# One GpSimd weight split a tile in the first mixture, and a shorter, padded balancing loop in the second routing

## The chip, the core and the metric

The kernel runs on one core of a Trainium2 chip. A core has five engines with queues of their own: TensorE (PE in the rows; its weight loads are PEld), VectorE (DVE), ScalarE (ACT), GpSimd (POOL) and SyncE (SP, which only issues transfers here). The metric is device time in microseconds (us).

## The reference, cut to what matters

Three layers follow each other: attention whose scores under a row's threshold are dropped, a mixture of eight experts in which every token goes to the expert of its largest logit, and a second mixture in which (token, expert) pairs are taken in falling order of their logits and each expert takes at most 288 tokens.

```python
e_idx = np.argmax(logits, axis=1)                  # first mixture
h = np.maximum(x[mask] @ w1[e], 0.0)
out[mask] = gate_w[mask, None] * eom[mask, e, None] * (h @ w2[e])
...
cap = N // E                                       # second mixture: 2304 // 8
order = np.argsort(-logits.flatten())
for idx in order:
    tok, e = idx // E, idx % E
    if assigned[tok] >= 0 or counts[e] >= cap: continue
    assigned[tok] = e; counts[e] += 1
out[mask] = np.maximum(x[mask] @ w1[e], 0.0) @ w2[e]
```

## The kernel before

All work is in program order on each engine; the order is written out by hand in Python, and engines wait for each other by semaphores that the framework places.

**First mixture (`moe1`).** The tokens are sorted by expert into tiles of 128; with these inputs tiles 0 to 22 run (tiles 23 and 24 stand in a branch that is not taken). A tile needs eight weight chunks of 128 x 1024: c = 0 to 3 for the first product (`mm1`), c = 4 to 7 for the second (`mm2`). Products are made in split precision: `split(t,c)` makes `wh`, a rounded copy of the raw chunk (ScalarE, L609), and `wl`, the rest raw - wh (a subtraction, L610 on GpSimd or L611 on VectorE). Which engine subtracts is the condition in L610: before, GpSimd does c = 2 from tile 3 on, c = 5 from tile 1 on and c = 7 from tile 2 on; VectorE does the others. Once `wl` is there, SyncE's `prefetch` may load the next expert's chunk into the same buffer.

`splits(n)` lets the splits run up to n chunks ahead of those TensorE has used, and seven buffers hold split chunks. Worked out from `order` and from the calls of `splits`, an iteration t of the steady loop puts this into VectorE's queue: the splits (t,4), (t,5), (t,6); then `ey(t-1)`, which scales the second product of the tile before out of PSUM into `y` (L667); then two `hl` (L650, low parts of the turned activations, out of PSUM); then the splits (t,7), (t+2,0); then `xl` (L621, out of PSUM); then the splits (t+2,1), (t+2,2), (t+2,3). Of these, the ones that GpSimd makes go into its queue instead, between its `gather` calls (L615, indirect loads of tokens). TensorE's queue in the same iteration: the first half of `mm1(t+1)`, the transposes `Th` of `hT(t)` (L647), the second half of `mm1(t+1)`, the transposes `Ty` of `y` (L673), the transposes `Tx` of the next tokens (L619), `mm2(t)` (L660 to L662), and in every second iteration the next router's logits. In tile t = 20 to 22 `reach` adds a maximum over all logits, with a small copy `fmb` (L696) on VectorE.

**Second routing (`route2`).** Six iterations look for each expert's threshold at once. In each, VectorE compares the current scores with 33 levels (`G`, L832), TensorE counts (`cn`, 25 small products, L836), VectorE marks the levels whose count is at least 288 (`gp`), TensorE sums the marks of each expert onto all partitions (`sp`, L858), and VectorE derives a step `s` and a factor `f` from `sp` (L861, L862, L864, L866; 8 columns each), shifts and scales the scores (`D`, `Qe`, `U`) and takes the new choice `O`. Beside it, in iterations 1 to 4 (counted from 0), TensorE and ScalarE split weight chunks of the second mixture (`split_pe`, two half chunks an iteration, written to `Tw`), and `busy(n)` issues n products of 512 columns whose result nobody reads. After the loop `rows` ranks the chosen tokens (26 products, L876 and L877), builds one-hot rows (`OT`, `OR`) and multiplies them into token indices (L900), with which GpSimd gathers the tokens of the first expert (L995).

**Second mixture (`moe2`).** It begins with `busy(10)` (L1043), then transposes the gathered tokens (L1001) and multiplies, eight experts with three tiles of 96 tokens each.

Of the kernel before, what the change touches and what calls it, by code (L numbers as in the profile page):

```python
# [9 lines left out]
F32 = mybir.dt.float32  # L10
F32R = mybir.dt.float32r
BF16 = mybir.dt.bfloat16
I32 = mybir.dt.int32
AF = mybir.ActivationFunctionType
ALU = mybir.AluOpType
AX = mybir.AxisListType
ET = mybir.EngineType
P = 128
# [24 lines left out]
class Route:  # L43
# [8 lines left out]
    def T(self, nm, sh, dt=F32):  # L52
        return self.p.tile([P]+sh,dt,name=nm)
# [506 lines left out]
def moe1(tc, K, r, rts, xd, w1, w2, wg2, ys, LG2, reach_, ahead):  # L560
# [3 lines left out]
    nc=tc.nc; ident=K['ident']; N=NT1  # L564
    with ExitStack() as ctx:
# [7 lines left out]
        def rv(c,par): return raw[c][:,ds(par,1),:].rearrange("p a f -> p (a f)")  # L573
# [25 lines left out]
        def prefetch(t,c):  # L599
            q=regs[t]; nc.sync.dma_start(rvd(c,q['o']),src(q['n'],c),cond=q['c'],cond_hint=(t%3==0))  # L600
# [6 lines left out]
        def split(t,c):  # L607
            q=regs[t]; h,l=wtile()
            nc.scalar.copy(h,rv(c,q['a']))  # L609
            if t>(2 if c==2 else 0 if c==5 else 1 if c==7 else N): nc.gpsimd.tensor_sub(l,rv(c,q['p']),h.bitcast(F32))  # L610
            else: nc.vector.tensor_sub(l,rv(c,q['v']),h.bitcast(F32))  # L611
            prefetch(t,c); W[t,c]=(h,l)
        def gather(t):
# [97 lines left out]
        def splits(ahead):  # L711

            nonlocal pos
            while pos<min(used+ahead,ends[cur[0]]):
                t,c=order[pos]; pos+=1
                if c==0: regload(t)
                if t==0 and c<6: prefetch(t,c)
                else: split(t,c)
# [58 lines left out]
def route2_ahead(tc, K, A, ix, vs):  # L777

    V=tc.nc.vector; T=lambda nm,sh,dt=F32: K['cst'].tile([P]+sh,dt,name=nm)
    inv=T("inv",[1]); V.tensor_scalar_max(inv,A,1.0e-30); V.reciprocal(inv,inv); V.tensor_scalar_mul(inv,inv,KC/1.5)  # L780
    vb=T("vb",[NT1]); V.tensor_scalar(vb,vs,1.0,-1.0,op0=ALU.subtract,op1=ALU.mult)
    i2=T("i2",[2,NT1],I32); V.tensor_scalar(i2[:,0],ix,4,None,op0=ALU.arith_shift_right); V.tensor_scalar(i2[:,1],ix,15,None,op0=ALU.bitwise_and)
    f3=T("f3",[2,NT1]); V.tensor_copy(f3,i2)
    return vb,f3,inv


def route2(tc, K, LG2, A, ix, vs):
# [9 lines left out]
    nc=tc.nc; cst=K['cst']; V=nc.vector; g=nc.gpsimd; ident=K['ident']; K1=KC+1  # L797
    it2=K['it2']
    with ExitStack() as ctx:
        def pool(name,bufs,space=None):  # L800
            return ctx.enter_context(tc.tile_pool(name=name,bufs=bufs,side='right',reuse_waits="tile",**({'space':bass.MemoryType.PSUM} if space else {})))
        p=pool("r2",1)
        T=lambda nm,sh,dt=F32: p.tile([P]+sh,dt,name=nm)
        M8=lambda a: a.unsqueeze(2).to_broadcast([P,NT1,8])
        E8=lambda a: a.unsqueeze(1).to_broadcast([P,NT1,8])
        OH=T("OH",[26,8],BF16); g.memset(OH[:,25],0.0); O=OH[:,:NT1]
        Q=T("Q",[NT1,9]); g.memset(Q[:,:,8:9],0.5); Qe=Q[:,:,:8]

        rtile=yield
        vb,f3,inv=route2_ahead(tc,K,A,ix,vs)  # L810
        mn=T("mn",[NT1]); U=T("U",[NT1,8]); D=T("D",[NT1,8]); u=T("u",[NT1]); G=T("G2",[NT1,K1],BF16)
# [9 lines left out]
        def want0(w=ALL): s_=slice(*w); V.tensor_reduce(mn[:,s_],Q[:,s_],axis=AX.X,op=ALU.min)  # L821
        def want1(w=ALL): s_=slice(*w); V.tensor_tensor(O[:,s_],Qe[:,s_],W(mn,w,8),op=ALU.is_equal)
        def begin(w):
            s_=slice(*w)
            V.scalar_tensor_tensor(Qe[:,s_],LG2[:,s_],-TINY,W(vb,w,8),op0=ALU.mult,op1=ALU.add)
            V.tensor_scalar(U[:,s_],LG2[:,s_],A,inv,op0=ALU.add,op1=ALU.mult)
            want0(w); want1(w)
# [9 lines left out]
        def counts(cn,w):  # L837
            for z in looks(w): count((cn,*w),z)
# [5 lines left out]
        split,fetch=yield  # L844
        ps=pool("r2p",2,1)
        begin((EARLY,NT1))
        gp=p.tile([K1,8],BF16,name="gp"); s=T("s",[8]); f=T("f",[8]); f1=T("f1",[8]); f2=T("f2",[8])
        def busy(n):

            w=ps.tile([P,512],F32,tag="s",name="w")  # L850
            for _ in range(n): nc.tensor.matmul(w,K['onesb'],K['onesb'].unsqueeze(1).to_broadcast([P,4,P]),start=True,stop=True)
        def iteration(extra=0,warm=0,first=False):

            cn=ps.tile([K1,8],F32,tag="s",name="cn")
            counts(cn,(EARLY,NT1) if first else ALL)
            if first: V.scalar_tensor_tensor(gp,cn,287.5,nA,op0=ALU.subtract,op1=ALU.is_ge)
            else: V.tensor_scalar(gp,cn,287.5,None,op0=ALU.is_ge)
            sp=ps.tile([P,8],F32,tag="s",name="sp"); nc.tensor.matmul(sp,K['onesb'][:K1],gp,start=True,stop=True)  # L858
            for _ in range(extra): next(split)
            if warm: busy(warm)  # L860
            V.tensor_scalar(s,sp,1.0,0.0,op0=ALU.subtract,op1=ALU.max)  # L861
            V.tensor_scalar(f1,sp,KC+0.5,0.5-ZOOM,op0=ALU.is_ge,op1=ALU.mult)  # L862
            V.tensor_sub(D,U,E8(s))
            V.tensor_scalar(f2,sp,0.5,1.0-ZOOM,op0=ALU.is_lt,op1=ALU.mult)  # L864
            V.scalar_tensor_tensor(Qe,D,0.0,Qe,op0=ALU.is_lt,op1=ALU.add)
            V.scalar_tensor_tensor(f,f1,ZOOM,f2,op0=ALU.add,op1=ALU.add)  # L866
            want0()
            V.tensor_mul(U,D,E8(f))
            want1()
        ee=T("ee",[NT1]); sa=T("sa",[NT1,8]); rk=T("rk2",[NT1]); rw=T("rw",[NT1]); q1=T("q1",[NT1]); q2=T("q2",[NT1]); tt=T("tt",[NT1])  # L870
        OT=T("OT",[NT1,4,24],BF16); OR=T("OR",[NT1,96],BF16); sc=T("sc",[2,24]); Rr=[None]; n8=T("n8",[8]); dn=T("dn",[8]); fl=T("fl",[1]); fi2=T("fi2",[1],I32)
# [2 lines left out]
        def ranks():  # L874
            r=Rr[0]=ps.tile([P,26,8],F32,tag="R",bufs=1,name="R")
            nc.tensor.matmul(r,K['tri'],OH,start=True,stop=False,skip_group_check=True)  # L876
            for c in range(NT1): nc.tensor.matmul(r[:,c+1:],K['onesb'],OH[:,c:c+1].to_broadcast([P,NT1-c,8]),start=False,stop=c==NT1-1,skip_group_check=True)  # L877
        def rows(flag):

            ranks()  # L880
            V.tensor_mul(D,O,io8); V.tensor_reduce(ee,D,axis=AX.X,op=ALU.add)
            V.tensor_scalar_mul(e3,vb,-99.0); V.scalar_tensor_tensor(e3,ee,3.0,e3,op0=ALU.mult,op1=ALU.add)
            r=Rr[0]
            V.tensor_mul(sa,r[:,:25],O)
            if flag: V.tensor_scalar(dn,r[:,25],288.0,None,op0=ALU.not_equal)
            V.tensor_reduce(rk,sa,axis=AX.X,op=ALU.add)
            if flag: V.tensor_reduce(fl,dn,axis=AX.X,op=ALU.max)
            V.tensor_scalar(q1,rk,95.5,None,op0=ALU.is_ge)
            if flag: V.tensor_copy(fi2,fl)
            V.scalar_tensor_tensor(q2,rk,191.5,q1,op0=ALU.is_ge,op1=ALU.add)  # L890
            V.tensor_add(tt,e3,q2)
            V.scalar_tensor_tensor(rw,q2,-96.0,rk,op0=ALU.mult,op1=ALU.add)
            def hot(eng,t0,t1): eng.tensor_tensor(OR[:,t0:t1],io96[:,:96].unsqueeze(1).to_broadcast([P,t1-t0,96]),rw[:,t0:t1].unsqueeze(2).to_broadcast([P,t1-t0,96]),op=ALU.is_equal)
            V.tensor_tensor(OT[:,:,2],K['iota'][:,:24].unsqueeze(1).to_broadcast([P,NT1,24]),b24(tt),op=ALU.is_equal)
            io96=ps.tile([P,96],F32,tag="s",name="io96"); V.tensor_copy(io96,K['iota'][:,:96])
            g.tensor_mul(OT[:,:,0],OT[:,:,2],b24(K['iota'][:,:NT1]))
            nc.scalar.activation(OT[:,:,1],OT[:,:,2],AF.Copy,scale=K['pf'])
            for t in (0,5,10,15,20): hot(V,t,t+5)
            IX=ps.tile([96,2,24],F32,tag="s",name="IX2")
            for c in range(NT1): nc.tensor.matmul(IX,OR[:,c],OT[:,c,0:2],start=c==0,stop=c==NT1-1)  # L900
            V.tensor_copy(sc[:96],IX)
            V.scalar_tensor_tensor(it2[:96,0],sc[:96,0],128.0,sc[:96,1],op0=ALU.mult,op1=ALU.add)
# [8 lines left out]
        def greedy(c8):  # L911
# [18 lines left out]
                V.tensor_scalar(pen,pen,NBIG,None,op0=ALU.mult)  # L930
                V.tensor_add(L,L,M8(pen)); V.tensor_add(L,L,E8(cl))
            V.tensor_copy(O,oh)
        for j in range(6): iteration(2 if 1<=j<5 else 0,0 if j<5 else 5,j==0)
        rows(True); fetch(False)
        flag=lambda: nc.values_load(fi2[0:1,0:1],min_val=0,max_val=1)>0

# [13 lines left out]
def moe2(tc, K, ys, w1, w2, out):  # L950
# [3 lines left out]
    nc=tc.nc; ident=K['ident']  # L954
    with ExitStack() as ctx:
# [41 lines left out]
        def xT(e,i):  # L997
            if i==0: XT[e]=(xp.tile([P,4,288],F32R,tag="xh",name="xh"),xp.tile([P,4,288],F32R,tag="xl",name="xl"))
            h,l=XT[e]; x=X.pop((e,i)); s=slice(i*96,i*96+96)
            p=psT.tile([P,4,96],F32,tag="T",name="Tx")  # L1000
            for c in range(4): nc.tensor.transpose(p[:,c].bitcast(F32R),x[:,c*P:(c+1)*P],K['identr'][:96,:96])  # L1001
            nc.scalar.copy(h[:,:,s],p); nc.vector.tensor_sub(l[:,:,s],p,h[:,:,s].bitcast(F32))  # L1002
# [37 lines left out]
        def busy(n):  # L1040

            w=psT.tile([P,512],F32,tag="T",name="w")
            for _ in range(n): nc.tensor.matmul(w,K['onesb'],K['onesb'].unsqueeze(1).to_broadcast([P,4,P]),start=True,stop=True)  # L1043
        busy(10)
        for i in range(3): xT(0,i); busy(3 if i<2 else 2)
        splits(6); loads(14)
        for e in range(8):
# [83 lines left out]
```

## Time and profile before

| | |
|---|---|
| median of 3 runs | 946.09 us (945.7 to 946.3) |
| the profiled execution's own time | 945.42 us |
| its span, first to last instruction | 943.6 us |
| mean granted TensorE clock | 0.981 of full speed |
| busy: PE, DVE, ACT, POOL | 886.3, 725.2, 635.6, 384.7 us |

The span is what the rows are placed in: times in them are us from its start. Attention fills it to about 321 us, the first mixture to 657, the second routing to 704, the second mixture the rest. An engine's busy time is an average over stages with different limits, so it is read by stage.

### The profile page before, as it was taken

The numbers are of one execution on the slowest core, as the hardware profiler recorded it, in microseconds if no ns is written. First come the engines' busy times: TensorE is split into PE (matmuls) and PEld (weight loads), VectorE is DVE, ScalarE is ACT, GpSimd is POOL, SyncE is SP. The second block draws the span as 40 slices with busy tenths as digits, with TensorE's granted clock in tenths as the row PEclk, the third lists the DMA queues.
The fourth block names the chain that finished last, engine by engine and source line by source line (L and its number), as shares of the span: only waits on it lengthen the run. The fifth ranks groups of instructions, "written<-read, shape, count | busy, mean of one in ns | idle before, by whom it ended". The sixth has DMA issues, their size and how long they took to land. (4 is left out here: it accounts for less than half of the span.)

```text
span 943.6 us, 18044 instructions
## 1 busy us (share of the span) xinstructions
PE 886.3 (94%) x5939; PEld 733.2 (78%) x5939; DVE 725.2 (77%) x1191; ACT 635.6 (67%) x1070; POOL 384.7 (41%) x391
## 2 busy tenths in 40 slices
PE   7899999999999999899999999998779999999995
PEld 6677777777777667678787777786449999999994
DVE  5898988888888789798999998987755555555540
ACT  5787878878977677677787788774315555555541
POOL 4234323433431324577777776774030221122211
PEclk9999999999999999999999999999779999999998
DMA  7534444544331670155544655111535666666500
GB/s 190 149 88 124 122 118 115 130 128 115 104 83 53 221 259 25 44 163 185 170 154 148 211 168 182 43 36 46 180 117 180 194 192 186 179 193 203 162 26 25
DMA packets 69346, 127.64 MB, mean 135 GB/s; under 512 B 14912, under 2 KB 27200, under 8 KB 69248
## 3 DMA queue, kind: packets, MB, share of 16 engines
q1 hardware_dynamic: 64016, 109.91, 38.4%
q0 software_dynamic: 5232, 16.52, 5.6%
q8 instruction: 49, 0.80, 0.4%
q14 instruction: 49, 0.40, 0.1%
HBM read 159.70 MB, written 15.99 MB: 186 GB/s over the span
## 5 line engine op out<-in xcount | busy, mean ns | idle before, releaser
L611 DVE TENSOR_TENSOR wl<-raw,wh 128x1024 fp32r<-128x1024 f32 x115 | 218.1, 1916 | 28.4 <-ACT wh L609 28.1
L610 POOL TENSOR_TENSOR wl<-raw,wh 128x1024 fp32r<-128x1024 f32 x63 | 167.6, 2662 | 102.2 <-ACT wh L609 101.4
L609 ACT CAST wh<-raw 128x1024 fp32r x178 | 177.7, 1064 | 4.0 <-PE Y L662 3.3
L469 ACT ACTIVATE e<-S,nm 128x576 f32<-128x576 f32 x144 | 107.8, 749 | 55.0 <-DVE nm L464 54.6
L464 DVE TENSOR_REDUCE nm<-S 128x1 f32<-128x576 f32 x144 | 108.4, 757 | 21.8 <-PE S L388 10.6
L499 DVE SCALAR_TENSOR_TENSOR a<-S,th,e 128x576 f32<-128x576 f32 x144 | 114.4, 814 | 11.1 <-ACT e L469 4.8
L966 DVE TENSOR_TENSOR wl<-raw,wh 128x1024 fp32r<-128x1024 f32 x60 | 73.4, 1225 | 36.9 <-ACT wh L966 36.9
L1037 POOL DMA_INDIRECT out_dram<-o,it x24 | 22.4, 934 | 173.0 <-ACT o L1031 154.1
L397 PE MATMUL T<-ident,a 128*128 128x128 f32 x576 | 86.6, 273 | 0.0
L1008 PE MATMUL H<-xh,wh 128*128 128x288 f32 x256 | 77.8, 304 | 0.1
L1020 PE MATMUL Y<-hh,wh 128*128 128x288 f32 x256 | 77.5, 303 | 0.0
L318 POOL TENSOR_TENSOR ql<-f,QH 64x512 fp32r<-64x512 f32 x30 | 38.2, 1274 | 94.5 <-ACT f L317 76.4
L419 PE MATMUL O<-aT,v 128*64 128x288 f32 x512 | 75.8, 418 | 0.5 <-ACT xt L424 0.5
L1009 PE MATMUL H<-xl,wh 128*128 128x288 f32 x256 | 75.6, 295 | 0.2 <-DVE xl L1002 0.2
L633 PE MATMUL H<-wh,xh 128*128 128x512 f32 x184 | 75.1, 408 | 0.7 <-ACT xh L621 0.7
L1021 PE MATMUL Y<-hl,wh 128*128 128x288 f32 x256 | 75.5, 295 | 0.0
L1022 PE MATMUL Y<-hh,wl 128*128 128x288 f32 x256 | 75.5, 295 | 0.0
L402 ACT COPY aT<-T 128x512 f32<-128x512 f32 x128 | 75.2, 588 | 0.2 <-PE T L397 0.2
L660 PE MATMUL Y<-wh,hh 128*128 128x512 f32 x184 | 74.5, 405 | 0.9 <-ACT wh L609 0.9
L1010 PE MATMUL H<-xh,wl 128*128 128x288 f32 x256 | 75.3, 294 | 0.0
L662 PE MATMUL Y<-wh,hl 128*128 128x512 f32 x184 | 72.3, 393 | 0.0
L661 PE MATMUL Y<-wl,hh 128*128 128x512 f32 x184 | 72.3, 393 | 0.0
(344 smaller groups left out, 2130.4 us busy)
## 6 DMA issues: line engine op xcount, KB each, us to landing
raw<-in_moe_w_dram SPq DMA_DIRECT2D x256, 512.0 KB
ys<-y SPq DMA_DIRECT2D x23, 256.0 KB
q<-in_q_dram SPq DMA_DIRECT2D x16, 256.0 KB
k<-in_k_dram SPq DMA_DIRECT2D x16, 256.0 KB
v<-in_v_dram SPq DMA_DIRECT2D x16, 256.0 KB
QA<-QH SPq DMA_DIRECT2D x32, 128.0 KB
QB<-QH SPq DMA_DIRECT2D x32, 128.0 KB
xd<-xr SPq DMA_DIRECT2D x16, 256.0 KB
```

The costliest lines, as they stand in the source:

```text
L397: for kb in (2*part,2*part+1): nc.tensor.transpose(TT[n][:,kb,:],a[:,o+kb*P:o+(kb+1)*P],ident)
L419: nc.tensor.matmul(O[hd*64:hd*64+64,:288],L['v'][:,hd,kb,:],aT[hd][:,kb,cs],start=kb==0,stop=False,skip_group_check=True)
L464: nc.vector.tensor_reduce(nm[:,i:i+1],S[i][:,:,:288],axis=AX.XY,op=ALU.max,negate=True)
L469: nc.scalar.activation(e[i],S[i][:,:,:288],AF.Exp,bias=nm[:,i:i+1])
L499: nc.vector.scalar_tensor_tensor(a[:,hd*576:hd*576+576].rearrange("p (a b) -> p a b",a=2),S[i][:,:,:288],th[:,i:i+1],e[i],op0=ALU.is_ge,op ...
L609: nc.scalar.copy(h,rv(c,q['a']))
L610: if t>(2 if c==2 else 0 if c==5 else 1 if c==7 else N): nc.gpsimd.tensor_sub(l,rv(c,q['p']),h.bitcast(F32))
L611: else: nc.vector.tensor_sub(l,rv(c,q['v']),h.bitcast(F32))
L1008: nc.tensor.matmul(H[:,:288],wh[:,fs],xh[:,kc],start=kc==0,stop=False)
L1009: nc.tensor.matmul(H[:,:288],wh[:,fs],xl[:,kc],start=False,stop=False)
L1020: nc.tensor.matmul(Y[:,:288],wh[:,ds_],h,start=f==0,stop=False)
L1021: nc.tensor.matmul(Y[:,:288],wh[:,ds_],l,start=False,stop=False)
```

## The change

In the first mixture GpSimd makes one subtraction a tile: c = 5 in tile 1, c = 6 in later tiles. All others go to VectorE.

In the second routing a constant matrix `SF` is written once by GpSimd. Two products of its columns with `gp`, into two halves of `sp`, now give the step and the factor less one; the four small VectorE instructions that derived `s` and `f` go, and `D` and `U` read `sp` in PSUM. Three `busy` counts change: 3 more in iteration 4, 8 new after the ranks, and 16 for 10 ahead of the second mixture.

```diff
-            if t>(2 if c==2 else 0 if c==5 else 1 if c==7 else N): nc.gpsimd.tensor_sub(l,rv(c,q['p']),h.bitcast(F32))
+            if t>0 and c==(5 if t==1 else 6): nc.gpsimd.tensor_sub(l,rv(c,q['p']),h.bitcast(F32))
             else: nc.vector.tensor_sub(l,rv(c,q['v']),h.bitcast(F32))
...
+        SF=p.tile([K1,2,P],BF16,name="SF"); g.memset(SF[:,0],1.0); g.memset(SF[:1,0],0.0)
+        g.memset(SF[:,1],0.0); g.memset(SF[:1,1],ZOOM-1.0); g.memset(SF[KC:K1,1],0.5-ZOOM)
...
-            sp=ps.tile([P,8],F32,tag="s",name="sp"); nc.tensor.matmul(sp,K['onesb'][:K1],gp,start=True,stop=True)
+            sp=ps.tile([P,2,8],F32,tag="s",name="sp")
+            for x in range(2): nc.tensor.matmul(sp[:,x],SF[:,x],gp,start=True,stop=True)
             for _ in range(extra): next(split)
             if warm: busy(warm)
-            V.tensor_scalar(s,sp,1.0,0.0,op0=ALU.subtract,op1=ALU.max)
-            V.tensor_scalar(f1,sp,KC+0.5,0.5-ZOOM,op0=ALU.is_ge,op1=ALU.mult)
-            V.tensor_sub(D,U,E8(s))
-            V.tensor_scalar(f2,sp,0.5,1.0-ZOOM,op0=ALU.is_lt,op1=ALU.mult)
+            V.tensor_sub(D,U,E8(sp[:,0]))
             V.scalar_tensor_tensor(Qe,D,0.0,Qe,op0=ALU.is_lt,op1=ALU.add)
-            V.scalar_tensor_tensor(f,f1,ZOOM,f2,op0=ALU.add,op1=ALU.add)
             want0()
-            V.tensor_mul(U,D,E8(f))
+            V.scalar_tensor_tensor(U,E8(sp[:,1]),1.0,D,op0=ALU.add,op1=ALU.mult)
             want1()
...
             ranks()
+            if flag: busy(8)
...
-        for j in range(6): iteration(2 if 1<=j<5 else 0,0 if j<5 else 5,j==0)
+        for j in range(6): iteration(2 if 1<=j<5 else 0,(0,0,0,0,3,5)[j],j==0)
...
-        busy(10)
+        busy(16)
```

## Rows read from the trace of the kernel before

**Rows 1.** Busy us by stretch: PE, PEld, DVE, ACT, POOL (instructions), PEclk, DMA share, GB/s

```profile
382.00:383.00 1.00, 1.00 (x4) 0.81 (x3) 1.00 (x2) 1.00 (x2) 0.00 (x0) 0.50 0.78 293
...
510.00:540.00 30.00, 29.71 (x153) 23.95 (x152) 27.65 (x21) 23.84 (x31) 22.46 (x10) 1.00 0.61 208
...
720.00:740.00 20.00, 20.00 (x162) 19.99 (x161) 9.63 (x14) 9.26 (x17) 0.94 (x1) 1.00 0.45 134
```

**Rows 2.** TensorE's waits, 390 to 650 us: total, times, longest

```profile
PE Ty L673 <- DVE y L667: 2.0, 9, 0.2
PE Tx L619 <- DVE hl L650: 1.9, 2, 1.4
```

**Rows 3.** Groups by line, 380 to 665 us: busy, mean ns, idle before

```profile
L611 DVE TENSOR_TENSOR wl<-raw,wh 128x1024 fp32r<-128x1024 f32 x97 | 190.6, 1979 | 26.6 <-ACT wh L609 26.3
```

**Rows 4.** VectorE's timeline around tiles 1 and 2: start, length, operation

```profile
355.18 4.62 DVE L611 TENSOR_TENSOR wl<-raw,wh 128x1024 fp32r<-128x1024 f32 x4
...
367.40 12.32 DVE L611 TENSOR_TENSOR wl<-raw,wh 128x1024 fp32r<-128x1024 f32 x5
379.65 0.74 DVE L667 TENSOR_SCALAR y<-Y,gs 128x512 f32<-128x512 f32 x1
```

**Rows 5.** GpSimd's timeline, the same stretch

```profile
368.44 2.43 POOL L610 TENSOR_TENSOR wl<-raw,wh 128x1024 fp32r<-128x1024 f32 x1 [3.85 <-ACT wh L609]
...
376.01 2.63 POOL L610 TENSOR_TENSOR wl<-raw,wh 128x1024 fp32r<-128x1024 f32 x1 [0.67 <-ACT wh L609]
```

**Rows 6.** ScalarE's timeline, the same stretch

```profile
370.82 2.94 ACT L609 CAST wh<-raw 128x1024 fp32r x3
```

**Rows 7.** TensorE's timeline, the same stretch; idle before in brackets

```profile
380.53 0.63 PE L673 MATMUL Ty<-ident,y 128*128 128x128 f32 x4 [3.46 <-DVE y L667]
...
381.44 0.76 PE L660 MATMUL Y<-wh,hh 128*128 128x512 f32 x1
...
384.89 0.39 PE L662 MATMUL Y<-wh,hl 128*128 128x512 f32 x1
```

**Rows 8.** VectorE's timeline in later tiles

```profile
422.12 0.74 DVE L667 TENSOR_SCALAR y<-Y,gs 128x512 f32<-128x512 f32 x1
422.78 1.27 DVE L650 TENSOR_TENSOR hl<-Th,hh 128x512 fp32r<-128x512 f32 x2
...
425.46 0.68 DVE L621 TENSOR_TENSOR xl<-Tx,xh 128x512 fp32r<-128x512 f32 x1
...
639.13 1.42 DVE L696 COPY fmb<-fm 1x128 f32<-1x128 f32 x1
```

**Rows 9.** GpSimd's timeline beside the first of them

```profile
421.75 2.70 POOL L610 TENSOR_TENSOR wl<-raw,wh 128x1024 fp32r<-128x1024 f32 x1 [0.63 <-ACT wh L609]
```

**Rows 10.** TensorE's timeline in later tiles, two iterations apart

```profile
423.01 0.63 PE L673 MATMUL Ty<-ident,y 128*128 128x128 f32 x4 [0.22 <-DVE y L667]
...
449.99 0.63 PE L673 MATMUL Ty<-ident,y 128*128 128x128 f32 x4 [0.21 <-DVE y L667]
```

**Rows 11.** VectorE in the second routing

```profile
673.53 0.17 DVE L861 TENSOR_SCALAR s<-sp 128x8 f32<-128x8 f32 x1 [0.25 <-PE sp L858]
...
673.74 0.37 DVE L863 TENSOR_TENSOR D<-U,s 128x200 f32<-128x200 f32 x1
...
674.14 0.37 DVE L865 SCALAR_TENSOR_TENSOR Q<-D,Q 128x200 f32<-128x200 f32 x1
...
692.64 0.37 DVE L884 TENSOR_TENSOR sa<-R,OH 128x200 f32<-128x200 f32 x1 [1.17 <-PE R L877]
```

**Rows 12.** TensorE in the second routing and at the head of the second mixture

```profile
671.57 0.80 PE L974 MATMUL Tw<-wh,identm 128*128 128x512 f32 x1
672.30 0.79 PE L836 MATMUL cn<-OH,G 128*33 128x8 bf16 x25
...
699.33 3.73 PE L1043 MATMUL w<-onesb 128*128 128x512 bf16 x10 [0.69 <-PEq L937]
704.16 0.53 PE L1001 MATMUL Tx<-identr,x 96*128 96x96 f32 x4 [1.10 <-DMA x<-ys,it]
```

More of the change, by code (lines that the diff above doesn't have):

```diff
@@ L846, in route2 @@
         begin((EARLY,NT1))
-        gp=p.tile([K1,8],BF16,name="gp"); s=T("s",[8]); f=T("f",[8]); f1=T("f1",[8]); f2=T("f2",[8])
+        gp=p.tile([K1,8],BF16,name="gp")
         def busy(n):
```

## The prediction

> **What bounds the kernel now.** First read the busy times by stretch. In a steady stretch of the first mixture TensorE is busy 29.71 of 30 us, and in the second mixture 20.00 of 20 [rows 1]. VectorE has 27.65 of 30 us in the first and GpSimd 22.46 [rows 1]. So TensorE is the bound in both, and a change of the subtractions pays only where TensorE waits for VectorE. TensorE's list of waits says where that is: between 390 and 650 us nine short waits for `y`, 2.0 us in all, and two for `hl`, 1.9 us, of which one is 1.4 [rows 2]. Ahead of that stretch one wait is larger than all of these: in tile 2 `Ty` stands 3.46 us idle for `y` [rows 7]. After it the clock is at 0.50, the 1.2 GHz level [rows 1]. The gap before it is the only idle time in the stretch.
>
> VectorE's timeline tells why `y` is late. Four subtractions with GpSimd quiet take 4.62 us, 1.155 each; the five ahead of `y` take 12.32 us, 2.46 each [rows 4]. Beside those five GpSimd makes three of its own, the first from 368.44, the last from 376.01 to 378.64 [rows 5]. Five at 1.155 are 5.8 us, so 6.5 us were lost to three subtractions of about 2.5 us each: I read it as the two engines' subtractions taking turns, a whole instruction at a time. What reads PSUM is not held up: `y` ran 0.74 us inside a GpSimd subtraction of 2.70 (421.75 to 424.45) [rows 8, 9], as long as after the third one had ended [rows 4].
>
> **The change part by part: the first mixture.** GpSimd loses two of its three subtractions a tile, VectorE gets them. Hand walk of tile 2 with the queue order of the code, from the same start, 367.40 [rows 4]: VectorE makes (3,0) to (3,3), all four now, at 1.155, to 372.0. ScalarE's copies for (2,4), (2,5), (2,6) end at about 371.8, 372.8 and 373.8 [rows 6], so VectorE makes (2,4) to 373.2 and (2,5) to 374.35. Then comes `y`, because (2,6) is GpSimd's: it is done at about 375.1 instead of 380.4. TensorE was ready for it at 380.53 - 3.46 = 377.07 [rows 7], so the wait goes, 3.46 us. What is late next: `hl` needs 1.27 us behind `y` and is ready at 376.4; GpSimd's (2,6) runs from 374.35 to about 376.8 under `y` and `hl`, which read PSUM; (2,7) follows to about 378.0, and the second product, which uses it last, would start at 377.07 + (381.44 - 380.53) = 378.0 and needs (2,7) more than 3 us later. Nothing takes the wait's place. The slow clock behind it goes too: from 381.44 nine products, to the start of the one at 384.89, took 3.45 us [rows 7]. At twice the clock they would take at best half, 1.7; some part of a start-to-start time may not scale, so I take 2.1 (bounds 1.7 and 3.45), a gain of 1.35, and for the eight transposes ahead of them, between 380.53 and 381.44, another 0.2. Tile 2: 5.0 us. Bounds: 0, if the turns are no turns, to 5.4.
>
> Later tiles. In the order of the code two subtractions stand ahead of `y` in VectorE's queue before and after; after, none of them has to take turns with GpSimd's (t,5). The nine waits of 0.2 us should go: 1.8 us. In tile 21 the copy `fmb` took 1.42 us, one row of 128 numbers, beside a GpSimd subtraction, and `hl` behind it made TensorE wait 1.4 [rows 2, 8]. There GpSimd's (21,6) will still be running when `fmb` comes, but by my walk VectorE gets to `y` some 2 us sooner, and the wait goes: 1.4 us, bounds 0 to 1.6.
>
> What the added work costs VectorE: seven at 1.155 are 8.1 us a tile, `hl`, `y` and `xl` 2.7 [rows 8], together 10.8. A tile lasts (449.99 - 423.01)/2 = 13.5 us [rows 10]. One GpSimd subtraction can hold VectorE up by 2.5 us at most, which makes 13.3: still hidden under TensorE, though by a hair. I take 11 to 12, since the GpSimd one falls under `y` and `hl`. ScalarE's copies, the loads and the gathers keep their number and order. Sum for the first mixture: 5.0 + 1.8 + 1.4 = 8.2 us saved.
>
> **The second routing.** Between the end of `sp` and `D` stand `s` and the first part of `f`: `D` starts 673.74 - 673.53 = 0.21 us after `s` [rows 11]. The other two small ones are worth nothing: `Qe` starts at 674.14, just when `D`, which it needs, has ended (674.11) [rows 11], so the small one in between filled a wait. That bounds the gain to 0 to 6 x 0.21 = 1.26 us. It is not had where TensorE comes last: in iteration 2 the counts start at 672.30, behind a weight split from 671.57 of 0.80 us [rows 12], and iteration 4 has the same clock phase; so I count four of six, 0.84. Against it stands the second product. The 25 counts take 0.79 us with their weight loads, 0.03 each [rows 12]; if `D` waits for both products, six cost 0.2; as the upper bound one could take the delay of a whole small instruction, 0.16, six times 1.0. I take 0.25, nearest to the counts. The memsets of `SF` are GpSimd's and come when it has nothing else.
>
> `D` and `U` now read `sp` from PSUM. `sa` reads 200 columns of PSUM in 0.37 us, `D` on SBUF takes 0.37 [rows 11], so I cost that at nothing. The Trainium skill speaks against it: Perfetto Trace Analysis, section Optimizing Scalar/DVE Operations, gives VectorE about 60 ns of overhead an instruction on SBUF and about 125 on PSUM. By that rule the sum would be about 0.8 us worse (estimate from that page: twelve instructions at 65 ns). Here the rows decide, and they show no difference.
>
> The dummies. Ten of them ran 3.73 us from 699.33, to 703.06, and the gathered tokens let TensorE go on at 704.16, after 1.10 idle [rows 12]. 512 columns are 0.43 us at 1.2 GHz and 0.21 at 2.4, and the mean of the ten is 0.37, so some three of them ran at the upper level, which I place last. Six more end at 704.3 (all at the upper level) to 705.6 (all at the lower). I take 0.2 us of cost, bounds 0.1 to 1.5. The 8 after the ranks stand where TensorE has nothing to do until the one-hot rows are made, the 3 of iteration 4 between the splits and the counts. They may leave the ranks and L900 at the higher clock; I take 0.3 us for that, bounds -0.3 to 0.9.
>
> Sum for the routing: 0.84 - 0.25 - 0.2 + 0.3 = 0.7 us saved. Altogether 8.9 us off a span of 943.6: 934.7. The execution's own time was 945.42, 1.8 more than its span, and the median of the runs is 946.09, 0.7 above that: 934.7 + 1.8 + 0.3 (half the distance) = 936.8.
>
> **The rivals.** *Another wait takes the place of the tile-2 wait* (its products wait for tokens or for `hl`, or the clock falls all the same): the gain of tile 2 is 0 to 2, the time 940 to 942. For it: the stretch is crowded, with ScalarE copying in long rows [rows 6]. Against it: the walk leaves over 1 us for each.
>
> *The routing gives back*: the dummies hold TensorE past the tokens (1.5) and the second product costs its upper bound (1.0): 2.2 us worse than my sum, 939.
>
> *VectorE becomes the bound in the first mixture*: slower. A subtraction on VectorE takes 1.98 us on average now [rows 3]. If that is not turns but a general slowness beside GpSimd, loads and ScalarE, seven take more than a tile allows as soon as their mean is above (13.5 - 2.7)/7 = 1.54 us. At 1.7 a tile is 1.1 us longer, over 20 tiles 22 us: 959 with the rest. For it: 27.65 of 30 us busy before [rows 1]. Against it: 1.155 each wherever GpSimd is quiet [rows 4].
>
> *It does nothing*: the short waits stay and the clock costs what it cost, within 2 us of 946.1.
>
> **How the numbers follow.** Forecast 0.62, tile 2 filled otherwise 0.15, routing gives back 0.10, VectorE the bound 0.07, nothing 0.06. Faster by over 0.2%, which is about what a measurement of this kernel can tell from no change (1.9 us): 0.62 + 0.15 + 0.10 = 0.87; within it 0.06; slower 0.07. The range leaves out the slower cases and takes in the others: below the forecast 3 us (the upper bounds of the routing, 1.26 + 0.9 without the costs, and the waits' bounds), above it to 942.5.
>
> **What would show it.** VectorE's mean subtraction falls from 1.98 to 1.3 us or less with about 137 instead of 97 in that stretch; `Ty` in tile 2 has no idle time in front and the clock stays at full speed to 386; the nine waits are gone; the first mixture ends some 8 us sooner; `D` follows `sp` directly, and `Tx` of the second mixture still waits for its tokens, not for dummies. I am wrong if VectorE shows no idle time in the steady stretch, or if `Tx` starts right behind `busy(16)`.

## The result and the profile after

The changed kernel takes 932.76 us (median; 929.19 to 934.29) against 946.19 (945.7 to 947.32) for the kernel before on the same chip: ratio 0.9851, 95% interval 0.9831 to 0.9872, 13.4 us less. The forecast was 936.8 with a range from about 3 us below it to 942.5: the direction was right and the gain lies where it was looked for, in the first mixture, but it was larger than the range allowed. The profiled execution is the slowest of its four: 934.29 us, with a span of 932.3 against 943.6.

The views that answer to those of before follow in the same order. First the busy times by stretch (answering [rows 1]; columns as there):

```profile
382.00:383.00 1.00, 1.00 (x5) 0.56 (x3) 1.00 (x2) 0.00 (x0) 0.00 (x0) 1.00 0.00 0
510.00:540.00 30.00, 30.00 (x156) 24.59 (x155) 25.43 (x27) 24.64 (x33) 8.54 (x4) 1.00 0.51 176
```

VectorE makes far more subtractions and is busy for less time, 25.43 of 30 us instead of 27.65. The groups by line, 380 to 665 us, say why (answering [rows 3]): the mean falls from 1979 to 1258 ns, while GpSimd's own stays long.

```profile
L611 DVE TENSOR_TENSOR wl<-raw,wh 128x1024 fp32r<-128x1024 f32 x135 | 163.0, 1258 | 22.1 <-ACT wh L609 19.4 <-DMA raw<-in_moe_w_dram 0.3
L610 POOL TENSOR_TENSOR wl<-raw,wh 128x1024 fp32r<-128x1024 f32 x20 | 58.3, 2916 | 167.1 <-PE Th L647 86.7 <-ACT wh L609 60.8 <-issue 19.5
```

TensorE's waits, 390 to 650 us (answering [rows 2]): the nine short ones for `y` are gone, and there is a new one of 1.1 us in tile 22 (the list names `A`, a small copy that stands right behind `y` in VectorE's queue). The other two belong to the last tile, which lay behind 650 us before.

```profile
PE Ty L673 <- DVE A L698: 1.1, 1, 1.1
PE Ty L673 <- DVEq L765: 1.0, 1, 1.0
PE L L689 <- issue: 0.7, 1, 0.7
```

Tile 2 on VectorE's timeline (answering [rows 4]):

```profile
367.53 6.89 DVE L611 TENSOR_TENSOR wl<-raw,wh 128x1024 fp32r<-128x1024 f32 x6
374.34 0.74 DVE L667 TENSOR_SCALAR y<-Y,gs 128x512 f32<-128x512 f32 x1
375.00 1.28 DVE L650 TENSOR_TENSOR hl<-Th,hh 128x512 fp32r<-128x512 f32 x2
376.20 2.72 DVE L611 TENSOR_TENSOR wl<-raw,wh 128x1024 fp32r<-128x1024 f32 x2
```

GpSimd's timeline beside it (answering [rows 5]):

```profile
373.98 2.71 POOL L610 TENSOR_TENSOR wl<-raw,wh 128x1024 fp32r<-128x1024 f32 x1 [9.44 <-ACT wh L609]
```

and TensorE's (answering [rows 7]):

```profile
376.42 0.39 PE L635 MATMUL H<-wh,xl 128*128 128x512 f32 x1
376.65 0.60 PE L673 MATMUL Ty<-ident,y 128*128 128x128 f32 x4
...
377.38 0.46 PE L660 MATMUL Y<-wh,hh 128*128 128x512 f32 x1
```

Six subtractions take 6.89 us, 1.15 each, where five took 12.32. `y` starts at 374.34 instead of 379.65, under GpSimd's one subtraction, and `Ty` starts with no idle time in front.

**Where the time went.** The start of `Ty` marks each tile, so the distances between such rows show where the 11.3 us of span went. Worked out from the starts of `Ty` in both traces (tile by tile, us):

| stretch | before | after | gain | forecast |
|---|---|---|---|---|
| `Ty` of the first tile to the third (holds tile 2's wait) | 10.83 + 15.52 | 6.81 + 13.44 | 6.1 | 5.0 |
| third to twenty-first, 18 distances | 243.10 | 235.99 | 7.1 | 1.8 |
| twenty-first to last, 2 distances | 9.57 + 8.90 | 9.15 + 10.26 | -0.9 | 1.4 |
| last `Ty` to the first `Tx` of the second mixture (routing) | 46.54 | 47.35 | -0.8 | 0.7 |

They add up to 11.5; the first `Ty` itself comes 0.1 later. The 10.26 is of this execution: in the four other profiled kernels with the same first mixture it is 8.63 or 8.64, so this profile shows 1.6 us less gain than they do. The large surprise is the second line.

The steady loop is best read at the same tile in both. Before, `Ty` at 423.01 is the row of [rows 10], with 0.22 us idle listed in front. TensorE's timeline around it, before:

```profile
422.40 0.39 PE L635 MATMUL H<-wh,xl 128*128 128x512 f32 x1
...
423.51 0.54 PE L619 MATMUL Tx<-identr,x 128*128 128x128 f32 x4
424.11 0.44 PE L684 MATMUL Tl<-ident,ls 128*128 128x128 f32 x2
424.30 0.48 PE L660 MATMUL Y<-wh,hh 128*128 128x512 f32 x1
```

and after:

```profile
416.07 0.40 PE L635 MATMUL H<-wh,xl 128*128 128x512 f32 x1
416.31 0.60 PE L673 MATMUL Ty<-ident,y 128*128 128x128 f32 x4
416.67 0.54 PE L619 MATMUL Tx<-identr,x 128*128 128x128 f32 x4
417.04 0.40 PE L684 MATMUL Tl<-ident,ls 128*128 128x128 f32 x2
417.20 0.48 PE L660 MATMUL Y<-wh,hh 128*128 128x512 f32 x1
```

From the last `H` product to the first `Y` product it is 1.90 us before and 1.13 after: 0.77 lost, of which the list of waits showed 0.22. From `L635` to `Ty` 0.61 against 0.24: 0.37. `Ty` to `Tx` 0.50 against 0.36 and `Tx` to `Tl` 0.60 against 0.37: another 0.37, the rest at `Y`. The second part has its cause in [rows 8]: the two `hl` stand behind the late `y` in VectorE's queue, 422.78 to 424.05, and `Tx` and `Tl` start as the first and the second end. In the code `Th`, `Ty`, `Tx` and `Tl` take turns in the buffers of one PSUM tag, so a late `hl`, which reads `Th`, is a late buffer. And `y` is late for the same reason as in tile 2: the subtraction ahead of it takes its turn with GpSimd's. VectorE's timeline before shows it,

```profile
419.52 2.68 DVE L611 TENSOR_TENSOR wl<-raw,wh 128x1024 fp32r<-128x1024 f32 x1 [0.67 <-ACT wh L609]
```

with GpSimd's beside it:

```profile
418.63 2.49 POOL L610 TENSOR_TENSOR wl<-raw,wh 128x1024 fp32r<-128x1024 f32 x1 [2.68 <-ACT wh L609]
```

Nowhere else in the 106 rows of TensorE's timeline for these two tiles do before and after drift apart by more than 0.04 us. So each pair of tiles took 27.0 us (13.80 and 13.20) and takes 26.22 (13.43 and 12.79): nine pairs at 0.78 are the 7.1.

The list of what TensorE's weight loads wait for would have pointed there. Before, 390 to 650 us:

```profile
PEld Ty L673 <- ACT wh L609: 5.5, 9, 0.6
...
PEld Tl L684 <- DVE hl L650: 2.1, 10, 0.2
```

5.5 and 2.1 make 7.6, near the 7.1 gained; after, the first row is gone and the second is 0.2 us, once. The list is a pointer and no price: a single wait is 0.6 and 0.2 in it, where the two parts lost 0.37 and 0.40. (The first row names ScalarE's copies; in the tile shown the last of them ended at 422.61 and `y` at 422.86, just ahead of `Ty`'s first weight load at 422.98.)

### The profile page after: what moved, and what is told of

The parts are those of the page before. It is cut to its first block, busy times and chain, and to the rows that moved or that the text cites. A ratio compares the mean times of both kernels' runs of the same rounds, so it can differ in the third digit from the quotient of the medians.

```text
span 932.3 us, 18078 instructions
## 1 busy us (share of the span) xinstructions
PE 884.7 (95%) x5962; PEld 735.0 (79%) x5962; DVE 696.7 (75%) x1208; ACT 633.2 (68%) x1070; POOL 272.9 (29%) x355
## 5 line engine op out<-in xcount | busy, mean ns | idle before, releaser
L611 DVE TENSOR_TENSOR wl<-raw,wh 128x1024 fp32r<-128x1024 f32 x156 | 187.9, 1255 | 24.2 <-ACT wh L609 21.4
L609 ACT CAST wh<-raw 128x1024 fp32r x178 | 175.8, 1068 | 0.8 <-DMA raw<-in_moe_w_dram 0.5
L610 POOL TENSOR_TENSOR wl<-raw,wh 128x1024 fp32r<-128x1024 f32 x22 | 63.4, 2883 | 197.9 <-ACT wh L609 91.7
L968 DVE TENSOR_TENSOR wl<-raw,wh 128x1024 fp32r<-128x1024 f32 x60 | 73.4, 1225 | 36.8 <-ACT wh L968 36.8
L635 PE MATMUL H<-wh,xl 128*128 128x512 f32 x184 | 72.2, 392 | 0.0
```

## The experiments

Each experiment changes one of the two kernels where it says so. Its ratio is to the kernel before, run beside it on the same chip, with a median there of 945.86 to 946.86 us.

**Only the condition of the subtractions.** The kernel before with one line changed:

```diff
-            if t>(2 if c==2 else 0 if c==5 else 1 if c==7 else N): nc.gpsimd.tensor_sub(...)
+            if t>0 and c==(5 if t==1 else 6): nc.gpsimd.tensor_sub(...)
```

> Only the first mixture's condition is changed. Theory A (all of the gain, and more, was made in the first mixture: in the two profiles the first sp of the second routing comes 12.3 us earlier, and from there to the end the changed kernel loses 1.0): 946.2 - 12.3 = 933.9 us, ratio 0.987, and the two-tile pitch of Ty 26.2 us instead of 27.0. Rival B (the first mixture gave the 8.2 us that I predicted and the routing the rest): 938 us.

931.94 us (931.27 to 932.54), ratio 0.984 (0.9823 to 0.9857). That is the whole gain, and `Ty`'s distances are those of the changed kernel, to 0.01 but for the last (Ty 3 to 21: 235.98).

**Only the second routing.** All else of the change, with the old condition in L610:

> Only the second routing and the dummies are changed; the first mixture is as before. Theory A: 946.2 + 1.0 = 947.2 us (loop 1.0 longer, ranks 0.9 shorter, the 16 dummies 0.9 longer). Rival B: 942 us, the rest of the measured 13.4 us after 8.2 in the first mixture. My prediction's sum for this part alone: 945.5.

946.68 (944.62 to 949.49), ratio 0.9997 (0.9984 to 1.001): the routing's part is worth nothing that can be measured.

**No new dummies.** The changed kernel without `busy(8)`, with (0,0,0,0,0,5) in the loop and `busy(10)` at the head:

> The whole change without its new dummies (0 in iteration 4, none after the ranks, 10 at the head of the second mixture). Theory A (the products shorten each iteration that VectorE bounds by 0.19, four of six, and the dummies as a whole cost more than the ranks gain): 0.8 below the run with the split alone, 933.1 us. Rival C (the dummies pay, by keeping the clock up through ranks and index products): slower than the whole change, 934 to 935.

931.37 (930.88 to 931.85), ratio 0.9831 (0.9814 to 0.9847). The profiles part the chain from the dummies. The five distances of `gp` take 25.85 us in the first experiment (old chain) and 25.07 here, so by these two profiles the new chain saves 0.8. From the last `sp` to the token indices `it` it is 9.76 us here, without the eight dummies, and 9.76 in the changed kernel, with them.

**Ten at the head.** The changed kernel with one edit:

```diff
-        busy(16)
+        busy(10)
```

> The whole change, but 10 dummies at the head of the second mixture as before. Theory A (16 hold TensorE 0.9 us past the tokens): 0.9 us below the whole change, 931.9, and Tx waits for its tokens again. Rival C (the longer row of dummies saves slow products behind it): the same 932.8 or slower, with the clock at 0.50 in the first products of the second mixture.

930.9 (930.07 to 932.71), ratio 0.983 (0.9812 to 0.9848). TensorE's timeline of the changed kernel at the head of the second mixture:

```profile
687.12 6.07 PE L1045 MATMUL w<-onesb 128*128 128x512 bf16 x16 [0.69 <-PEq L939]
692.84 0.63 PE L1003 MATMUL Tx<-identr,x 96*128 96x96 f32 x4
```

and of this one:

```profile
684.67 4.45 PE L1045 MATMUL w<-onesb 128*128 128x512 bf16 x10 [0.69 <-PEq L939]
689.54 0.53 PE L1003 MATMUL Tx<-identr,x 96*128 96x96 f32 x4 [0.42 <-DMA x<-ys,it]
```

Sixteen hold TensorE past the arrival of the tokens, and `Tx` starts right behind them. From the making of the index list to `Tx` it is 6.1 us with sixteen and 5.2 with ten: 0.9 lost, with no gain behind it. The changed kernel's time (932.65 again below) is above those of the last two experiments by 1.3 to 1.8, which goes the same way, but the intervals overlap.

**The change again,** beside the next three:

> The whole change once more, beside the others on one chip. Theory A: 0.9 us above the run with 10 dummies at the head, 931.8 us; the intervals from Ty to Ty 13.43 and 12.79 us as in the first profile.

932.65 (931.72 to 934.39), ratio 0.9852 (0.983 to 0.9874). The last distance of `Ty` is 8.63 here, where the first profile had 10.26.

**Two chunks a tile on GpSimd.** The first experiment, with c = 2 left on GpSimd as before:

```diff
-            if t>0 and c==(5 if t==1 else 6): nc.gpsimd.tensor_sub(...)
+            if (t>0 and c==(5 if t==1 else 6)) or (t>2 and c==2): nc.gpsimd.tensor_sub(...)
```

> The split condition alone, but GpSimd also keeps c = 2 from tile 3 on: two subtractions a tile. Theory P (place: what costs is a GpSimd turn between the splits and y; c = 2 is done before the copies of (t,4) are there): as with one split, 932 us, pitch of two tiles 26.2 us. Theory Q (amount: each GpSimd subtraction costs its share): half of the steady gain lost, some 3.5 us more, 935.5.

938.41 (936.59 to 939.13), ratio 0.9907 (0.989 to 0.9924). My theory was that only the place matters, and c = 2 isn't ahead of `y`; it fell. Against the first experiment 6.5 us are lost: 4.0 in the steady loop (`Ty` 3 to 21 takes 240.02) and 2.0 around tile 2 (8.67 + 13.56 instead of 6.82 + 13.44). The pair of tiles takes 26.65 (13.65 and 13.0). VectorE's timeline in the tile that loses:

```profile
424.72 7.17 DVE L611 TENSOR_TENSOR wl<-raw,wh 128x1024 fp32r<-128x1024 f32 x3 [0.66 <-ACT wh L609]
431.81 0.74 DVE L667 TENSOR_SCALAR y<-Y,gs 128x512 f32<-128x512 f32 x1
432.47 1.27 DVE L650 TENSOR_TENSOR hl<-Th,hh 128x512 fp32r<-128x512 f32 x2
```

GpSimd's:

```profile
423.88 2.44 POOL L610 TENSOR_TENSOR wl<-raw,wh 128x1024 fp32r<-128x1024 f32 x1 [2.72 <-ACT wh L609]
427.67 3.13 POOL L610 TENSOR_TENSOR wl<-raw,wh 128x1024 fp32r<-128x1024 f32 x1 [1.35 <-ACT wh L609]
```

TensorE's:

```profile
432.16 0.39 PE L635 MATMUL H<-wh,xl 128*128 128x512 f32 x1
432.61 0.66 PE L673 MATMUL Ty<-ident,y 128*128 128x128 f32 x4
433.20 0.54 PE L619 MATMUL Tx<-identr,x 128*128 128x128 f32 x4
```

Three subtractions of VectorE beside GpSimd's two take 7.17 us, where GpSimd quiet they would take 3.5. So `y` ends at 432.55 and `Ty` starts at 432.61, 0.45 behind `L635` instead of 0.24, and `Tx` waits for `hl` again (0.59 instead of 0.36). The two losses, 0.21 and 0.23, are the pair's 0.43. GpSimd's subtraction needs no place ahead of `y`: it delays whatever VectorE subtracts beside it, and `y` comes behind that. The list of TensorE's own waits shows one wait for `y` in the whole stretch here, of 0.2 us; the weight loads' list shows nine, of 4.4 us, and ten of `Tx` for `hl`, of 1.8, which is more than the 4.0 that the loop lost.

**None on GpSimd.** The first experiment with `if t>N:`, so that VectorE makes all eight.

> The split condition alone, all subtractions on VectorE. Theory P: VectorE has 8 x 1.155 + 2.7 = 11.9 us of work in a tile of 13.1, y is done before TensorE asks for it: 931 to 932 us, and the wait in the last tiles for y behind GpSimd's (22,6) is gone. Rival R (VectorE becomes the bound without GpSimd's help, the slower rival of my prediction): waits for y in every tile, over 936 us.

932.11 (930.93 to 932.33), ratio 0.9841 (0.9823 to 0.9858). `Ty` 3 to 21 takes 235.99 us, as with one on GpSimd (235.98). This is the pace that TensorE's products set. VectorE has room for all of them: eight subtractions at 1.219 (the mean, 390 to 650 us) and 2.7 us for `hl`, `y` and `xl` are 12.5 of 13.1 us a tile. That the total is the same too is partly chance, since two differences outside the loop offset each other. The new wait of the last tiles goes (7.97 instead of 9.15). But in tile 1 the subtraction (1,5) now stands ahead of the first `y` in VectorE's queue, and the second product waits for that `y`. TensorE's timeline of the first experiment:

```profile
363.69 0.47 PE L660 MATMUL Y<-wh,hh 128*128 128x512 f32 x1 [0.86 <-ACT wh L609]
```

and of this one:

```profile
364.37 0.48 PE L660 MATMUL Y<-wh,hh 128*128 128x512 f32 x1 [1.52 <-DVE y L667]
```

From there to the first `Ty` it is 7.18 us here (371.55) instead of 5.53 (369.22): the granted clock was 0.61 between 364 and 368, where it was 1.00 in the first experiment. So tile 1 loses 2.3 us when GpSimd does not help there.

**`y` first.** The kernel before, with `ey(t-1)` ahead of the splits in VectorE's queue:

```diff
+                if t>t0 and not early: ey(t-1)
                 splits(5 if early else 7)
                 if nx: mm1(t+1,0,2)
                 if early: next(gates)
-                elif t>t0: ey(t-1)
```

> Before, with ey(t-1) moved ahead of the splits in VectorE's queue; GpSimd keeps its three. Theory P (a late y and hl is all that GpSimd's turns cost): most of the 0.78 us a pair comes back, 6 to 7 us in the later tiles, and in tile 2, where hl stays behind the splits, 1 to 2.5 of 6: 938 to 940 us. Theory Q (the amount of turns bounds VectorE): 946, the waits only move to hl.

942.19 (938.74 to 944.55), ratio 0.9953 (0.9938 to 0.9968), about a third of the gain. The place of `y` alone gets its part: tile 2's wait is gone (7.21 instead of 10.83), and `Ty` 3 to 21 takes 238.87, 4.2 less. But `hl` is now behind the splits: `Tx` in tile 2 waits 2.9 us for it, the next distance grows from 15.52 to 18.15, and the last two from 18.47 to 20.75. For the whole gain the turns with GpSimd have to go, not only their place in the queue.

The groups by line, 390 to 650 us, put these side by side. L611 on VectorE of the kernel before:

```profile
L611 DVE TENSOR_TENSOR wl<-raw,wh 128x1024 fp32r<-128x1024 f32 x94 | 185.8, 1991 | 25.6 <-ACT wh L609 25.3
```

with two chunks a tile on GpSimd:

```profile
L611 DVE TENSOR_TENSOR wl<-raw,wh 128x1024 fp32r<-128x1024 f32 x113 | 191.3, 1730 | 8.8 <-ACT wh L609 7.5
```

of the changed kernel:

```profile
L611 DVE TENSOR_TENSOR wl<-raw,wh 128x1024 fp32r<-128x1024 f32 x130 | 157.2, 1260 | 20.2 <-ACT wh L609 17.4 <-DMA raw<-in_moe_w_dram 0.3
```

with none on GpSimd:

```profile
L611 DVE TENSOR_TENSOR wl<-raw,wh 128x1024 fp32r<-128x1024 f32 x150 | 174.6, 1219 | 17.9 <-ACT wh L609 17.6 <-issue 0.2
```

Against 1219 ns each, VectorE lost 94 x 0.772 = 73 us to GpSimd's 58 subtractions, 1.25 each; 113 x 0.511 = 58 us to 38 with two a tile; and 130 x 0.041 = 5.3 us to 19 with one, 0.28 each. So one is nearly free where it falls under `y` and `hl`, which read PSUM, and the second costs VectorE (58 - 5.3) / 19 = 2.8 us, about its whole length (2.87 on average with two a tile). The Trainium skill, SBUF — State Buffer, section Who interferes with whom, states the rule behind it: a VectorE instruction with two SBUF inputs contends with a GpSimd instruction that reads SBUF, and the port pair that they share is an exclusive lock. The 2.8 us beside 2.87 agree.

**The last tile on VectorE.** Ten at the head, and

```diff
-            if t>0 and c==(5 if t==1 else 6): nc.gpsimd.tensor_sub(...)
+            if 0<t<22 and c==(5 if t==1 else 6): nc.gpsimd.tensor_sub(...)
```

> The whole change with 10 dummies at the head and with VectorE for all splits of tile 22. Theory (in the last tiles y waits behind GpSimd's turn for (22,6), as the run without GpSimd shows): the two last intervals from Ty to Ty 16.7 instead of 17.8 us, so 1.1 below the run with 10 at the head, 929.8 us. Rival (the wait moves to the second product's y): no difference, 930.9.

929.84 (928.68 to 931.68), ratio 0.9834 (0.9816 to 0.9851): the lowest median of all, though its interval overlaps with those of the changed kernel. It takes away the new wait of tile 22, which VectorE's timeline of the changed kernel explains:

```profile
629.91 4.53 DVE L611 TENSOR_TENSOR wl<-raw,wh 128x1024 fp32r<-128x1024 f32 x2
634.37 0.74 DVE L667 TENSOR_SCALAR y<-Y,gs 128x512 f32<-128x512 f32 x1
```

with GpSimd's beside it:

```profile
630.36 3.00 POOL L610 TENSOR_TENSOR wl<-raw,wh 128x1024 fp32r<-128x1024 f32 x1 [2.73 <-ACT wh L609]
```

At the end fewer chunks stand in the queues, and GpSimd's (22,6) comes beside VectorE's two splits ahead of `y` instead of under `y`: 4.53 us for the two. `Ty` at 635.23 waits 1.1. Without it the distance is 8.10 instead of 9.15.

**The loop kept warm.** The experiment before, with dummies (6,3,3,3,3,5) in the six iterations of the routing:

> The same, with 6, 3, 3, 3, 3, 5 dummies in the six iterations. Theory C (what lengthens two of the six iterations is TensorE at its lower level while it splits weights; more products keep it up): six iterations of about 4.7 us, sp to sp 23.5 us instead of 25.1 to 25.8, 928.2 us. Rival D (the dummies stand ahead of the counts, and the clock falls in the counts all the same): sp to sp 25 us or more, 930 or more.

932.22 (930.27 to 934.67), ratio 0.985 (0.9829 to 0.987): the gain expected did not come. The iteration that runs at the lower clock (0.51 from 655 to 660) got longer, 7.05 us instead of 5.20, mostly since its three dummies stand ahead of the counts and hold them up by 1.43; only from the third distance on are all 4.66 or 4.67. The profile is of the slowest of the four executions, and in it TensorE also stands still for 3.2 us between two dummies at the head, for no cause that the profile shows.

**The same with the old chain.** Dummies as above, `busy(8)` after the ranks, and the routing's chain of small operations as before:

> The same splits and dummies as the run before, with the old chain of four small VectorE instructions instead of the products. Theory P (each iteration that VectorE bounds loses the 0.19 us that the products save, now all six): 1.1 us above the run before, 929.3. Rival (the second product and the reads from PSUM take it back): the same time.

930.32 (929.42 to 933.71), ratio 0.9844 (0.9824 to 0.9865). The distances of `gp` where VectorE sets the pace are 4.85 here and 4.67 with the new chain: the old chain costs its 0.19 an iteration, and the total shows none of it (it is 1.9 us below the run before, with overlapping intervals).

**The weight splits spread.** The last-tile experiment, with the half chunks dealt otherwise:

```diff
-        for j in range(6): iteration(2 if 1<=j<5 else 0,(0,0,0,0,3,5)[j],j==0)
+        for j in range(6): iteration((0,1,2,2,3,0)[j],(0,0,0,0,0,5)[j],j==0)
```

> All of the change's numbers, but in the second routing the half weight chunks are dealt (0, 1, 2, 2, 3, 0) over the six iterations, where the change deals 2 to each of iterations 1 to 4; dummies only in the last iteration (5), ten products at the head, the last tile of the first mixture all on VectorE. Theory (a cold iteration is held by the two halves' products at 1.2 GHz, which stand ahead of the next counts): with one half of about 2.0 us in iteration 1 the work fits under VectorE's 4.7 us, so the iteration that took 5.2 to 5.85 us takes 4.7 to 4.9, the six counts lie 23.5 to 24.5 us apart, and the whole takes about 929. Rival (with less work ahead TensorE's clock stays low for longer, and another iteration is long in its place): 25 us or more, 930 or more.

930.75 (929.1 to 932.16), ratio 0.9835 (0.9815 to 0.9855). The first half of the theory held: the second distance is 4.71 instead of 5.20 to 5.85. The rival took the rest: the third is 5.74 and the fifth 6.42, and the six counts lie 26.2 us apart. Busy times by stretch in that kernel:

```profile
656.00:660.00 4.00, 3.73 (x31) 2.54 (x32) 3.18 (x12) 0.07 (x1) 0.00 (x0) 0.50 0.95 356
...
664.00:668.00 4.00, 2.99 (x33) 1.58 (x31) 3.38 (x12) 2.11 (x3) 0.00 (x0) 1.00 0.02 4
668.00:672.00 4.00, 4.00 (x8) 1.65 (x8) 3.66 (x12) 1.53 (x2) 0.00 (x0) 0.59 0.00 0
```

The granted clock was 0.50 until 660, was 1.00 from 664 to 668, where TensorE was busy 2.99 of 4 us, and fell again to 0.59, just in the iteration that now holds three half chunks.

## Why the prediction was right, and where it was wrong

**The step that failed is "The nine waits of 0.2 us should go: 1.8 us".** The waits went, and they were worth 7.1. Two things were missing. The listed idle time counts from the modelled end of the last product, 0.39 long, while products start 0.23 apart; from start to start the same wait was 0.37. And what was late next was left out: in these tiles I asked only about `y`, though `hl` stands right behind it in VectorE's queue and `Tx` and `Tl` wait for `hl`; the weight loads' list, which I did not read, points at these 0.40. The experiments bound it from both sides: with one subtraction on GpSimd and with none the loop runs at the same pace, 235.98 and 235.99, and with two it loses 0.43 a pair, at `Ty` and `Tx` and nowhere else.

**Tile 2** was right in mechanism and nearly in size: `y` was forecast to start at 374.35 and did at 374.34 (to the hundredth by luck: the row ahead of it began 0.13 later than in the walk), the clock stays at 1.00, no other wait takes the place. 5.0 forecast, 6.1 measured; 0.37 of that is a steady wait that falls into the second distance.

**Tile 21** was half right: 1.4 forecast, 0.7 in the experiment that changes the condition alone. `fmb` takes 1.47 us still, but no wait of TensorE for `hl` is left behind it; the new wait in tile 22 takes 1.05 back (9.15 against 8.10 without GpSimd's last subtraction).

**The turns** held: 1.26 us a subtraction instead of 1.98, and the reads of PSUM not held up. "I take 11 to 12" for VectorE's load was right too: 7 x 1.26 + 2.7 = 11.5.

**The routing** came out at nothing instead of 0.7. Its pieces: where VectorE sets the pace the distances of `gp` shrank from 4.86 to 4.67, as forecast, and the second product cost 0.03 (VectorE stands idle for 0.28 us between `gp` and `D`, where it was 0.25 between `gp` and `s`). So the chain gave 0.8, where I had 0.84 - 0.25 = 0.6. But two of the five distances are set by TensorE, not by VectorE. VectorE's timeline after shows it in the waits ahead of `gp`:

```profile
655.69 0.16 DVE L861 TENSOR_SCALAR gp<-cn 33x8 bf16<-33x8 f32 x1 [0.41 <-PE cn L840]
656.13 0.36 DVE L866 TENSOR_TENSOR D<-U,sp 128x200 f32<-128x200 f32 x1 [0.28 <-PE sp L863]
...
661.54 0.16 DVE L861 TENSOR_SCALAR gp<-cn 33x8 bf16<-33x8 f32 x1 [1.55 <-PE cn L840]
```

The iteration of 5.85 us holds its two halves at a clock of 0.50 (656 to 660), the last one of 5.87 at 0.62 (672 to 676) with three dummies more; without these it is 5.21, so they cost 0.7. First to last `sp` took 25.8 us instead of 24.8, but the chain is not to blame: with the new first mixture and the old chain it is 25.85. Nor did the eight dummies bring what I had hoped for. The counts of the ranks ran 1.35 us instead of 2.03 and 0.9 came back from the last `sp` to the index list, but the ranks run 1.35 in the first experiment and in the one without new dummies too. `busy(16)` took 0.9, where I had put 0.2 with a bound of 1.5. I had written that I was wrong if `Tx` started right behind `busy(16)`; it is what the profile shows. So the dummies, which I had put at 0.1 of gain in all, cost 1.6 in the profiles, more than the chain gave; the times of the whole kernel cannot tell the sum from nothing.

**Reading PSUM** cost VectorE nothing here: `D` took 0.36 us from `sp` in PSUM, 0.37 from SBUF [rows 11]. The rule of the Trainium skill, Perfetto Trace Analysis, section Optimizing Scalar/DVE Operations, which gives VectorE about 60 ns of overhead an instruction on SBUF and about 125 on PSUM, did not show in this operation, which has one of its two operands in PSUM.

**The rivals.** "VectorE becomes the bound" is refuted by the experiment with none on GpSimd. "The routing gives back" came true in its dummies, and was too small to matter beside the mis-sized term. What stays open: which of the routing's iterations are long moves with where the low clock falls, from kernel to kernel (5.82, 5.11 and 5.18 with the old chain, 5.83 and 5.87 with the new, 5.20 twice without the last tile's subtraction), and no arrangement tried here ends it.

## What to carry to other kernels

Price a short wait on a pipelined TensorE by the distance of its start from the start of the product in front, against the same pair where nothing waits, and add what is late behind the same producer; the weight loads' list shows where to look for both. A VectorE subtraction moved to GpSimd is no relief where both read SBUF: one a tile is nearly free if it falls under reads of PSUM, the second costs VectorE its whole length. Count dummy products ahead of an arrival by their length at the lower clock: here ten (4.45 us) ended before the tokens came, and sixteen (6.07) did not.

## What the runs showed that I had not expected

- Nine listed waits of 0.22 us cost 7.1 us in all, 0.78 for each.
- Eighteen distances take 235.98 and 235.99 us with seven or all eight subtractions on VectorE, 26.22 a pair; yet in tile 1 the one on GpSimd is worth 2.3 us, and in tile 22 its lack is worth 1.05. Before, at 27.0 a pair, TensorE counted as busy in 29.71 of 30 us: the 1% of idle time hid a loss of 2.9%.
- Sixteen products of 512 columns took 6.07 us, mostly at a granted clock near 0.5 (0.52 from 685 to 691), although eight others had run after the ranks at 1.00 (680 to 685).
